# One attention head per 64-row half of the TensorE array, with dense matmuls as pairs of halves, in a gated mix of a Fourier layer and sliding-window attention

## The chip, the cores and the metric

The kernel runs on one core of one Trainium2 chip. The metric is device time in microseconds (us) of one execution. A core has TensorE (PE, with its weight loads shown apart as PEld), VectorE (DVE), ScalarE (ACT), GpSimd (POOL) and SyncE (SP), which issues all DMAs of this kernel. Each engine works its own queue in order and waits for semaphores of the others.

## The reference

For one sequence of 2048 tokens and 512 features, a gate mixes a Fourier layer (a) and a sliding-window attention (b):

```python
x = A_x
g = sigmoid((x * gate_w).sum(-1, keepdims=True))
# a: real part of the DFT over features, then over the sequence
re, im = x @ dft_hid_re.T, x @ dft_hid_im.T
a = dft_seq_re @ re - dft_seq_im @ im
# b: 32 heads of 16 features, each query sees itself and the 255 keys before it
q, k, v = split(x @ wqkv)
p = softmax(where(0 <= i - j < 256, q @ k.T / 4, -1e9))
b = (p @ v) @ wo
return g * a + (1 - g) * b
```

The weights of q, k and v are scaled up, so scores are large and float32 accuracy is needed.

## The kernel before

**Dense matmuls.** Every dense product is exact to near float32 by splitting both factors into a rounded part `hi` and a rest `lo` (type float32r, which PE takes in one pass) and adding three products (`TERMS`). A step of contraction over 128 is so three matmuls of 128x128 weights by 512 columns. There are 2496 of them ahead of the output projection: projections of q and k (`dqk`, `qk_proj`), of v (`dv`, `v_proj`), the DFT over features (`dab`, `ab_proj`), and the DFT over the sequence (`dc`, `c_block` and `c_pair`, 16 row blocks for the real and 16 for the imaginary part, 48 matmuls each). A piece of the DFT matrix is loaded as `raw` (128x1024), cast to `hi` and subtracted to `lo` on DVE (`load_split`, lines 82 and 83), two pieces for each row block. The output projection (`wo_block`, 192 matmuls) follows when the attention is done.

**Attention.** Heads are taken in 4 groups of 4 pairs, and queries in blocks of 64 (`BQ`, `NB` = 32 blocks in a group, 128 block steps in all). One matmul serves both heads of a pair: 64 rows of its result belong to one head, 64 to the other. To keep the heads apart, the weights are copies of the block (`make_pad`, three on DVE at line 304 and one on ACT at line 302 for each block) in which half of the contraction rows is zeroed. For block n and pair p:

- `s_pair`: scores s of the block's queries against a window of up to 320 keys (PE, line 319). A custom reduction on DVE (line 321) adds the mask and takes the row's minimum of -s into `nm`; ACT (line 324) takes the exponential and its row sums `l`.
- every 8 blocks `m_rows` and `l_rows` transpose the maxima and the reciprocal sums on PE, and DMAs carry the maxima through DRAM into rows 96 to 99 of `ring[0]`, so that they become part of a contraction.
- `t_pair`, `LAG` = 18 blocks later: the scores transposed, t, of the block's keys against up to 320 queries, with the maximum subtracted by those rows (PE, line 384). ACT takes the exponential into `pt` (line 385), POOL zeroes what lies outside the window (lines 390 and 394).
- `pv`, for two blocks at a time: P times V in plain float32, four passes of PE, with 32 columns of weights for each pair, so that four column parts of the array are in use (line 411).

**Order.** PE's order is written out by hand: the loop over n and p issues one s, one t (`k = n - LAG`) and then takes dense matmuls from the generator `dense()` at a fixed rate (`fill`, `FILL_*` matmuls for each p). We call one p a slot: s, t and 3 or 4 dense matmuls. ACT, DVE, POOL and SP are ordered by the scheduler of the language. PSUM has eight buffers of 128x512: four (`ps_a`) that s and t, and the transposes, take in turn, two for P times V (`ps_o`), two for dense results (`ps_d`). A matmul into a buffer waits until what read the buffer before is done: for s that is the reduction on DVE, for t the exponential on ACT.

## Time and profile before

| | |
|---|---|
| Runs | 880.5, 881.56, 883.99 us (median 881.56) |
| The profiled execution, span | 881.0 us |
| Matmuls on PE in the profile | 5184 |
| First and last s (line 319) | 35.0 and 672.4 us |
| Last t (line 384) | 754.7 us |

The profile gives for each engine its busy time, for stretches of time the busy time of every engine, for groups of instructions their count, busy time and mean duration, and in a timeline the start, duration and (in brackets) the idle time ahead of single instructions with what ended it. Matmuls overlap in a pipeline, so the distance between starts tells more than the duration: a dense matmul lasts 0.39 us, and the next begins long before it ends. Up to 35 us the first projections run, then the attention with dense matmuls between, and behind 755 us what is left of the DFT and the output projection.

### The profile page before, as it was taken

What the parts mean: (1) busy time and instruction counts of PE and PEld (TensorE: products, weight loads), DVE (VectorE), ACT (ScalarE), POOL (GpSimd) and SP (SyncE); (2) the same over time, 40 slices, a digit from 0 to 9 for tenths busy, and PEclk for the clock granted to TensorE, in tenths of its full rate; (3) what the DMA queues carried; (4) which work ended last, traced back from release to release, by engine and by line L of the source; (5) the groups of instructions that cost most, each with busy time, mean ns of one, the idle gap of its engine ahead of it and who ended that gap; (6) DMA issues with size and microseconds to landing.
All of it is one profiled execution on the core that took longest, in us unless ns stands there. A gap on an engine that the chain in (4) does not pass through costs nothing.

```text
span 881.0 us, 17206 instructions
## 1 busy us (share of the span) xinstructions
PE 867.3 (98%) x5184; PEld 690.6 (78%) x5184; DVE 604.8 (69%) x1965; ACT 590.3 (67%) x1794; POOL 384.9 (44%) x1069
## 2 busy tenths in 40 slices
PE   7999899999999999999999999999999999999998
PEld 5888677777777778787878787878777787788886
DVE  4688789777888678787877677778786433544342
ACT  5488789878889887888888878888786444101000
POOL 9100165554544446656456565745555665100000
PEclk9999999999999999999999999999999999999999
DMA  7877667675656126544444454469743424355453
GB/s 246 274 232 212 197 218 263 216 246 179 225 198 213 43 72 216 159 130 126 140 141 132 147 147 128 134 203 324 256 154 95 137 96 144 110 180 165 134 160 113
DMA packets 89822, 152.13 MB, mean 173 GB/s; under 512 B 26752, under 2 KB 35456, under 8 KB 89728
## 3 DMA queue, kind: packets, MB, share of 16 engines
q1 hardware_dynamic: 89728, 151.02, 54.6%
q8 instruction: 41, 0.67, 0.3%
q14 instruction: 53, 0.43, 0.2%
HBM read 103.81 MB, written 47.19 MB: 171 GB/s over the span
## 4 chain that ended last, share of the span: by engine, by line
PE 93%; DVE 2%; DMA 2%; ACT 1%; issue 0%; SPq 0%; ACTq 0%
PE dc L442 40%; PE s L319 9%; PE dab L260 9%; PE t L384 8%; PE dqk L238 8%; PE o L411 8%; PE t L604 5%; PE dv L260 5%; DMA qk_scr<-hl 1%; DMA pt<-xT 1%; DMA ab_scr<-hl 1%; DVE sm L321 1%; ACT sm L324 0%; PE s L343 0%; PE s L331 0%
## 5 line engine op out<-in xcount | busy, mean ns | idle before, releaser
L442 PE MATMUL dc<-big,hi 128*128 128x512 f32 x1024 | 341.0, 394 | 0.0
L390 POOL TENSOR_SCALAR_AFFINE_SELECT pt<-pt 64x128 f32<-64x128 f32 x512 | 195.4, 382 | 285.2 <-ACT pt L385 270.1
L321 DVE CUSTOM_DVE_ANT_0 sm<-s,mask 128x320 f32<-128x320 f32 (+4 forms) x512 | 232.6, 462 | 114.6 <-PE t L384 74.9
L324 ACT ACTIVATE sm<-sm,nm 128x320 f32<-128x320 f32 (+4 forms) x512 | 276.6, 541 | 25.8 <-DVE nm L321 21.7
L385 ACT ACTIVATE pt<-t 128x320 f32<-128x320 f32 (+4 forms) x512 | 210.8, 414 | 117.9 <-PE t L384 114.4
L442 PEld LDWEIGHTS dc<-big,hi 128*128 128x128 f32 x1024 | 189.4, 188 | 28.1
L442 PE MATMUL dc<-big,lo 128*128 128x512 f32 x512 | 201.6, 394 | 0.0
L384 PE MATMUL t<-ring,pad 128*128 128x320 f32 (+4 forms) x512 | 158.3, 309 | 3.8 <-ACT pad L302 2.8
L319 PE MATMUL s<-ring,pad 128*128 128x320 f32 (+4 forms) x512 | 160.4, 313 | 0.8 <-ACT pt L385 0.8
L394 POOL TENSOR_SCALAR_AFFINE_SELECT pt<-pt 64x128 f32<-64x128 f32 x448 | 157.1, 351 | 0.0
L304 DVE TENSOR_SCALAR pad<-ring,half 96x256 fp32r<-96x256 f32 x384 | 122.3, 365 | 27.4 <-PE t L384 26.2
L319 PEld LDWEIGHTS s<-ring,pad 128*128 128x128 f32 x512 | 96.2, 188 | 41.5 <-issue 7.4
L384 PEld LDWEIGHTS t<-ring,pad 128*128 128x128 f32 x512 | 96.4, 188 | 27.8 <-issue 3.2
L442 PEld LDWEIGHTS dc<-big,lo 128*128 128x128 f32 x512 | 96.3, 188 | 11.2
L83 DVE TENSOR_TENSOR lo<-raw,hi 128x512 fp32r<-128x512 f32 x146 | 99.5, 709 | 0.2 <-ACT hi L80 0.2
L324 ACT ACTIVATION_READ_ACCUMULATOR sm<-sm,nm 128x1 f32 x512 | 97.8, 191 | 0.0
L260 PE MATMUL dab<-hi,big 128*128 128x512 f32 x256 | 86.6, 395 | 0.2 <-DVE hl L88 0.2
L82 DVE CAST hi<-raw 128x512 fp32r<-128x512 f32 x142 | 57.8, 444 | 39.2 <-DMA raw<-ci 19.6
L238 PE MATMUL dqk<-big,hi 128*128 128x512 f32 x240 | 84.2, 398 | 0.0
L80 ACT CAST raw<-ev 128x512 fp32r<-128x512 f32 x16 | 9.9, 621 | 108.5 <-DVE lo L83 64.9
L411 PE MATMUL o<-pt,vpad 128*32 128x320 f32 (+4 forms) x1408 | 78.4, 352 | 0.0
L411 PEld LDWEIGHTS o<-pt,vpad 128*32 128x32 f32 x1408 | 35.9, 109 | 37.5 <-issue 18.0
(79 smaller groups left out, 823.4 us busy)
## 6 DMA issues: line engine op xcount, KB each, us to landing
qk_scr<-hl SPq DMA_DIRECT2D x32, 512.0 KB
ring<-qk_scr SPq DMA_DIRECT2D x32, 512.0 KB
raw<-cr SPq DMA_DIRECT2D x32, 512.0 KB
raw<-ci SPq DMA_DIRECT2D x32, 512.0 KB
ab_scr<-hl SPq DMA_DIRECT2D x20, 512.0 KB
big<-ab_scr SPq DMA_DIRECT2D x20, 512.0 KB
ring<-qk_scr SPq DMA_DIRECT2D x32, 256.0 KB
r_scr<-ev SPq DMA_DIRECT2D x25, 256.0 KB
```

The costliest lines, as they stand in the source:

```text
L238: nc.tensor.matmul(ps, w[a][:, c:c + 128], XT[dk, ss][:, b], start=n == 0, stop=n == 11)
L260: nc.tensor.matmul(ps, XT[dk, ss][:, a, c * 128:(c + 1) * 128], wh[b], start=n == 0, stop=n == 11)
L304: nc.vector.tensor_scalar(dst, src, half[:96, h:h + 1], None, op0=OP.mult)
L319: nc.tensor.matmul(ps[:, :w], PAD[0, n][:, p], ring[1][:, p, k0:k0 + w], start=True, stop=True)
L321: mark("dve", nc.vector.tensor_tensor_reduce(out=sm[:, :w], in0=ps[:, :w], in1=mask[:, WIN - w:], scale=1.0, scalar=3e38, op0=OP.add, op1= ...
L324: mark("act", nc.scalar.activation(sm[:, :w], sm[:, :w], AF.Exp, bias=nm[:, c], scale=-1.0, accum_out=l[:, c]))
L384: nc.tensor.matmul(ps[:, :w], PAD[1, n][:, p], ring[0][:, p, q0:q0 + w], start=True, stop=True)
L385: nc.scalar.activation(pt[:, p, :w], ps[:, :w], AF.Exp, scale=-1.0)
L390: nc.gpsimd.affine_select(a, a, pattern=[[0, 2], [1, 64]], compare_op=OP.is_ge, fill=0.0, base=0, channel_multiplier=-1)
L394: nc.gpsimd.affine_select(a, a, pattern=[[0, 2], [-1, 64]], compare_op=OP.is_gt, fill=0.0, base=0, channel_multiplier=1)
L411: nc.tensor.matmul(OT[g, sb][32 * p:32 * p + 32, q - sb * 512:e - sb * 512], v2[:, p], pt[:, p, q - q0:e - q0], start=first, stop=kb == 8 ...
L442: nc.tensor.matmul(ps, w[a][:, s8 * 128:(s8 + 1) * 128], ab[SC[i]][:, b], start=i == 0 and a + b == 0, stop=i == 15 and a == 1)
```

## The change

Attention takes one head at a time. Heads come in 8 groups (`NS`) of 4 (`NH`), and queries in blocks of 128, so there are again 128 block steps. `ring[0]` and `ring[1]` hold two heads one above the other: head h of a pair has rows 64 h to 64 h + 63 of all tiles. Its matmuls contract over 48 or 50 of these rows, which uses one half of the array's rows; the windows are 384 wide. s of a slot has the half p % 2 and t the other one (`t_head(k, p ^ 1)`).

While the attention runs (`rows[0]`), every dense matmul is issued as two, one for each half of the contraction rows, into two PSUM buffers (`mm`, `acc`); `collect` adds them with a copy on ACT and an add on DVE, and where a result is added to something anyway, a second instruction does so. Results begun before the attention keep whole matmuls.

The padded copies, the masks for them, and the exponential of s with its row sums are left out. V's weights for a head have 16 columns of v and 16 of ones, so P times V gives the row sums in its row 16. `pv` runs once for 512 queries; its result is copied from PSUM by ACT, and the sums go through DRAM to DVE for the reciprocal, and through DRAM again to all rows. PSUM: three buffers (not four) for s, t and transposes, one for P times V, four for dense results. `LAG` is 9 blocks, of twice the size.

```diff
-BQ = 64
-NB = S // BQ
-WIN = 320
+NS = 8
+NH = 4
+NB = S // P
+WIN = 384
-LAG = 18
+LAG = 9
-FILL_FIRST, FILL_PROJ, FILL_SEQ = 3.0, 3.5, 3.6
+FILL_FIRST, FILL_PROJ, FILL_SEQ = 4.0, 4.2, 4.25
...
-    ps_a = ctx.enter_context(tc.tile_pool(name="ps_a", bufs=4, space=PSUM))
-    ps_o = ctx.enter_context(tc.tile_pool(name="ps_o", bufs=2, space=PSUM))
+    ps_a = ctx.enter_context(tc.tile_pool(name="ps_a", bufs=3, space=PSUM))
+    ps_o = ctx.enter_context(tc.tile_pool(name="ps_o", bufs=1, space=PSUM))
...
+    def acc():
+        return [ps_d.tile([P, 512], F32, name=f"d{h}", tag=f"d{h}", bufs=2) for h in range(1 + rows[0])]
+
+    def mm(pss, w, x, start, stop):
+        if len(pss) == 1:
+            nc.tensor.matmul(pss[0], w, x, start=start, stop=stop)
+        else:
+            for h in range(2):
+                r = slice(64 * h, 64 * h + 64)
+                nc.tensor.matmul(pss[h], w[r], x[r], start=start, stop=stop)
+
+    def collect(pss):
+        if len(pss) == 1:
+            return pss[0]
+        t = ev.tile([P, 512], F32, name="es", bufs=3)
+        mark("act", nc.scalar.copy(t, pss[0]))
+        mark("dve", nc.vector.tensor_add(t, pss[1], t))
+        return t
...
-    def s_pair(n, p):
+    def s_head(n, j):
+        p, h = divmod(j, 2)
...
+        k0 = max(0, (jb - 2) * P)
+        w = (jb + 1) * P - k0
+        r = slice(64 * h, 64 * h + 48)
         ps = ps_a.tile([P, 512], F32, name="s", tag="st")
-        nc.tensor.matmul(ps[:, :w], PAD[0, n][:, p], ring[1][:, p, k0:k0 + w], start=True, stop=True)
-        sm = at.tile([P, WIN], F32, name="sm", bufs=3)
+        nc.tensor.matmul(ps[:, :w], ring[0][r, p, jb * P:(jb + 1) * P], ring[1][r, p, k0:k0 + w],
+                         start=True, stop=True)
+        sm = at.tile([P, WIN], F32, name="sm")
         mark("dve", nc.vector.tensor_tensor_reduce(out=sm[:, :w], in0=ps[:, :w], in1=mask[:, WIN - w:],
                                                    scale=1.0, scalar=3e38, op0=OP.add, op1=OP.min,
-                                                   accum_out=nm[:, c]))
-        mark("act", nc.scalar.activation(sm[:, :w], sm[:, :w], AF.Exp, bias=nm[:, c], scale=-1.0,
-                                         accum_out=l[:, c]))
+                                                   accum_out=ML[u][:, c:c + 1]))
...
+    def t_head(n, j):
...
+        r = slice(64 * h, 64 * h + 50)
         ps = ps_a.tile([P, 512], F32, name="t", tag="st")
-        nc.tensor.matmul(ps[:, :w], PAD[1, n][:, p], ring[0][:, p, q0:q0 + w], start=True, stop=True)
-        nc.scalar.activation(pt[:, p, :w], ps[:, :w], AF.Exp, scale=-1.0)
+        nc.tensor.matmul(ps[:, :w], ring[1][r, p, q0:q0 + P], ring[0][r, p, q0:q0 + w], start=True, stop=True)
+        mark("act", nc.scalar.activation(pt[:, j, :w], ps[:, :w], AF.Exp, scale=-1.0))
...
+            for j in range(NH):
+                nc.tensor.matmul(ot[32 * j:32 * j + 32, a - sb * 512:e - sb * 512], v2[:, j],
+                                 pt[:, j, a - kb * P:e - kb * P], start=kb == kbs[0], stop=kb == kbs[-1],
                                  skip_group_check=True)
...
+        os = at.tile([P, 512], F32, name="os")
+        nc.scalar.copy(os, ot)
+        ls = l_scr[u]
+        ld(ls[0], os.rearrange("(j r) s -> j r s", r=32)[:, 16])
+        lt = at.tile([P, 16], F32, name="lt", bufs=1)
+        ld(lt, ls[0].rearrange("j (a b) -> (j a) b", b=16))
+        nc.vector.reciprocal(lt, lt)
+        ld(ls[1].rearrange("j (a b) -> (j a) b", b=16), lt)
+        rl = at.tile([P, 512], F32, name="rl", bufs=1)
+        ld(rl, bass.AP(tensor=ls.tensor, offset=ls[1].offset, ap=[[512, NH], [0, 32], [1, 512]]))
+        nc.vector.tensor_mul(rl, os, rl)
...
         for p in range(NH):
             if n < N:
-                s_pair(n, p)
+                s_head(n, p)
             if 0 <= k < N:
-                t_pair(k, p)
+                t_head(k, p ^ 1)
+                if p % 2:
+                    t_mask(k, p // 2)
             fill(n)
```

How the order of the engines changes is shown at two places. The first is PE in the middle of the attention, during the DFT over the sequence; before, a slot reads like this, with P times V (`o`) ahead of it (the numbers behind names count tiles):

```order
L411 MATMUL o<-pt,vpad_312 32x64 x4
L411 MATMUL o<-pt,vpad_312 32x256 x4
L411 MATMUL o<-pt,vpad_311 32x320 x4
L319 MATMUL s<-ring_252,pad_0_245 128x320
L384 MATMUL t<-ring_251,pad_0_248 128x320
L442 MATMUL dc<-big,hi 128x512
L442 MATMUL dc<-big,lo 128x512
L442 MATMUL dc<-big,hi 128x512 x2
L319 MATMUL s<-ring_252,pad_1_246 128x320
L384 MATMUL t<-ring_251,pad_1_249 128x320
```

And after (`d` are the dense results, two tiles for one result), two slots, with what each instruction waits for; here P times V is not shown:

```order
L305 MATMUL s<-ring_284,ring_283 128x384 [waits Activation_49]
L358 MATMUL t<-ring_283,ring_284 128x384 [waits DVE_49]
L202 MATMUL d_2166<-hi,big 128x512
L202 MATMUL d_2167<-hi,big 128x512
L202 MATMUL d_2166<-hi,big 128x512
L202 MATMUL d_2167<-hi,big 128x512
L202 MATMUL d_2166<-lo,big 128x512
L202 MATMUL d_2167<-lo,big 128x512
L202 MATMUL d_2166<-hi,big 128x512
L202 MATMUL d_2167<-hi,big 128x512
L305 MATMUL s<-ring_284,ring_283 128x384 [waits Activation_49]
L358 MATMUL t<-ring_283,ring_284 128x384 [waits DVE_49]
```

The operands of s and t are now the ring itself and not padded copies, dense matmuls stand in pairs, and with three buffers it is t that waits for DVE, and s for ACT. The second place is DVE in the DFT over the sequence, where pieces of the DFT matrix are split. Before (`sm,nm` is the reduction of s, with the row that reads its minimum behind it):

```order
L82 CAST hi<-raw 128x512 x2
L321 ISA sm,nm<-s,mask 128x320
L321 ISA nm 128x1
L83 TENSOR_TENSOR lo<-raw,hi 128x512 x2
L321 ISA sm,nm<-s,mask 128x320
L321 ISA nm 128x1
L304 TENSOR_SCALAR pad_1_246<-ring_251,half 96x4x64 x2
L304 TENSOR_SCALAR pad_1_249<-ring_252,half 96x4x64
L321 ISA sm,nm<-s,mask 128x320
```

After, at a like place (`ev` is the second half of a dense result):

```order
L308 ISA sm,nm<-s,mask 128x384
L308 ISA nm 128x1
L83 CAST hi<-raw 128x512 x2
L84 TENSOR_TENSOR lo<-raw,hi 128x512 x2
L532 SCALAR_TENSOR_TENSOR ev<-d_5505,g_305,ev 128x512
L308 ISA sm,nm<-s,mask 128x384
L308 ISA nm 128x1
L308 ISA sm,nm<-s,mask 128x384
L308 ISA nm 128x1
```

The padded copies are gone from between the reductions, and casts, subtractions and the second eviction of a dense result stand in one run between two of them.

## The prediction

> **What bounds the kernel now.** I read the head of the page, then the chain of waits, then one stretch of a hundred microseconds by engine.

> ```profile
> span 881.0 us, 17206 instructions
> PE 867.3 (98%) x5184; PEld 690.6 (78%) x5184; DVE 604.8 (69%) x1965; ACT 590.3 (67%) x1794; POOL 384.9 (44%) x1069
> PE 93%; DVE 2%; DMA 2%; ACT 1%; issue 0%; SPq 0%; ACTq 0%
> 400.00:500.00 100.00, 100.00 (x639) 79.01 (x638) 79.11 (x269) 82.10 (x255) 55.19 (x149) 1.00 0.44 135
> ```

> The last row gives span, then busy time of PE, PEld, DVE, ACT and POOL. PE has no gap while DVE and ACT are idle for a fifth: work taken from ACT, DVE or POOL alone is worth nothing here, and what counts is the time between starts on PE. The profiled 881.0 stands 0.56 under the median of 881.56, so the sum holds for both. The starts of one slot (one s, one t and its dense matmuls), in the timeline of PE:

> ```profile
> 405.56 0.31 PE L319 MATMUL s<-ring,pad 128*128 128x320 f32 x1
> 405.70 0.31 PE L384 MATMUL t<-ring,pad 128*128 128x320 f32 x1
> 405.86 0.63 PE L442 MATMUL dc<-big,hi 128*128 128x512 f32 x2
> 406.32 0.39 PE L442 MATMUL dc<-big,lo 128*128 128x512 f32 x1
> 406.55 0.40 PE L442 MATMUL dc<-big,hi 128*128 128x512 f32 x1
> 406.79 0.31 PE L319 MATMUL s<-ring,pad 128*128 128x320 f32 x1
> ```

> A dense matmul of 512 columns takes 0.235 from start to start (406.32 to 406.79, two), s or t of 320 columns 0.145 (405.56 to 405.86, two). Both are some 0.455 ns a column. A slot with four dense ones is 1.23.

> **s and t.** Columns of all s: 4 pairs x 4 groups x 9,600 = 153,600 of 320-wide windows (narrower at the edge), so s and t together cost 2 x 153,600 x 0.455 ns = 139 us. After, 184,320 columns each (384-wide), but s stands in one half of the rows and the t behind it in the other. If the halves run side by side, a pair costs what one does: 184,320 x 0.455 ns = 84, and 36 slots at each end have an s or a t alone, 36 x 0.175 = 6 more: 90. **Term: -49.** Not side by side it would be 168, +29. That parts of the array do run side by side, the P times V group shows, for column parts:

> ```profile
> L411 PE MATMUL o<-pt,vpad 128*32 128x320 f32 (+4 forms) x1408 | 78.4, 352 | 0.0
> 400.51 0.40 PE L442 MATMUL dc<-big,hi 128*128 128x512 f32 x1
> 400.83 1.29 PE L411 MATMUL o<-pt,vpad 128*32 128x64 f32 x24
> 402.05 0.41 PE L319 MATMUL s<-ring,pad 128*128 128x320 f32 x1
> 402.30 0.31 PE L384 MATMUL t<-ring,pad 128*128 128x320 f32 x1
> ```

> 1408 of 352 ns each fit into 78.4 us. No row of before shows row parts; I take them as overlapping likewise.

> **The dense matmuls.** 2364 of 2496 become pairs; 132 ahead of the first s and the 192 of the output projection stay whole. If a pair costs what the whole one did, 0.235, nothing changes, and that is the value I take. It can't be below, since each half streams the same 512 columns. Above, if the halves ran one after the other, 2364 x 0.235 = +555. Between lies the load of weights, which twice as many instructions now need. What one load takes at least, a short t shows:

> ```profile
> 751.02 0.19 PE L384 MATMUL t<-ring,pad 128*128 128x64 f32 x1
> 751.04 0.48 PE L442 MATMUL dc<-big,lo 128*128 128x512 f32 x1
> 751.37 0.63 PE L442 MATMUL dc<-big,hi 128*128 128x512 f32 x2
> ```

> From the t to the second dense one are 0.35; less 0.235 for the first dense one, the t took 0.115, though 64 columns are 0.03: that is the floor set by loading 128 columns of weights. Two loads in turn are 0.23, just inside a pair's 0.235, but s beside t would cost 0.23 in place of 0.175: 512 x 0.055 = +28, a rival below. Term: 0, with 0 to 555 as ends.

> [...]

> **P times V and the rows of maxima.** The batch of 640 columns above holds PE from 400.83 to 402.05, the dense one ahead lasts 0.32 in place of 0.235, and the s behind it 0.25 in place of 0.145: 1.41 in all, of which 640 x 4 passes x 0.455 ns = 1.17 (four column parts at once) is streaming and 0.24 the switch. Before, 64 batches of 600 columns in the mean: 64 x (1.09 + 0.24) = 85. After, 32 batches of 1440: 32 x (2.62 + 0.24) = 92. **Term: +7.** 33 transposes of maxima replace 16 of maxima and 16 of sums: 0.

> **What leaves ACT and DVE.** The second exponential with its row sums (L324), the padded copies (L302, L304) and their memsets go. PE waited for none of it in the stretch above, so this is 0. In return each dense result inside the attention is a copy on ACT and an add on DVE more, and the maximum covers 384 keys:

> ```profile
> L304 DVE TENSOR_SCALAR pad<-ring,half 96x256 fp32r<-96x256 f32 x384 | 122.3, 365 | 27.4 <-PE t L384 26.2 <-DMA ring<-qk_scr 1.0
> L321 DVE CUSTOM_DVE_ANT_0 sm<-s,mask 128x320 f32<-128x320 f32 x448 | 212.7, 483 | 100.6 <-PE t L384 73.8 <-PE s L319 22.0 <-ACT sm L324 3.3
> L321 DVE CUSTOM_DVE_ANT_0 sm<-s,mask 128x256 f32<-128x256 f32 x16 | 6.6, 418 | 2.1 <-PE t L384 1.1 <-PE s L319 0.6 <-ACT sm L324 0.4
> L88 DVE TENSOR_TENSOR hl<-dqk,hl 128x512 fp32r<-128x512 f32 x15 | 10.3, 684 | 2.2 <-ACT hl L86 2.2
> ```

> DVE: -122 for the pads; 65 ns more on 448 reductions (483 less 418 for 64 columns), +29; 69 adds and 32 second evictions at 0.68, +69; 32 products of 0.68 with the sums in place of 16, +11: within some 15 us of what it was. As a sum it still fits. When its work comes is another matter.

> **The wait that is added.** s and t took turns in four PSUM buffers and now have three. So t of slot p+1 lands in the buffer of s of slot p, and waits for that s's reduction; before, only the s two slots on did. Behind a waiting t on PE stand all dense pairs of the slot and the next P times V. The times:

> ```profile
> 409.00 0.31 PE L319 MATMUL s<-ring,pad 128*128 128x320 f32 x1
> 409.46 0.49 DVE L321 CUSTOM_DVE_ANT_0 sm<-s,mask 128x320 f32<-128x320 f32 x1 [0.53 <-PE t L384]
> 406.39 0.47 DVE L321 CUSTOM_DVE_ANT_0 sm<-s,mask 128x320 f32<-128x320 f32 x1
> 406.80 0.07 DVE L321 DVE_READ_ACCUMULATOR2_ANT nm<- 128x1 f32 x1
> 406.80 0.48 DVE L321 CUSTOM_DVE_ANT_0 sm<-s,mask 128x320 f32<-128x320 f32 x1
> 405.09 1.38 DVE L83 TENSOR_TENSOR lo<-raw,hi 128x512 fp32r<-128x512 f32 x2
> 403.82 0.94 DVE L82 CAST hi<-raw 128x512 fp32r<-128x512 f32 x2
> ```

> A reduction starts 0.46 after its s (409.00, 409.46) and holds DVE 0.41 (406.39 to 406.80); with 64 columns more 0.50 and 0.48, and its result stands 0.55 after its start. So s at 0 frees DVE at 0.98. If X is what DVE has in its queue before the next reduction, that one ends at 0.98 + X + 0.55. The t that needs it is due two slots after the first s, at 2 x (4 x 0.235 + 0.175) = 2.23, or up to 0.47 later where a slot holds five pairs (110 of 508 do). So X up to 0.65 to 0.9 costs nothing, and all above it stops PE. With four buffers it was one slot more, about 2.2.

> X from the order of DVE's queue: of 475 gaps between reductions behind the first 36, 228 are empty, 133 hold one instruction up to 0.65 (an lo is 1.30 / 2, a cast 0.4), 22 lie below 1.2, 38 between 1.2 and 1.9, and 54 above, 2.48 in the mean (two casts and two lo of a split piece are 2.1, with an add, product or eviction beside them 2.7 and more). At 0.65 all gaps together exceed the room by 133 us; the 54 alone, at 0.9, by 54 x 1.58 = 85. The ends are 0 (every gap finds PE late anyway) and 133; I take 85, since the middle gaps meet five-pair slots and P times V in part. **Term: +85.** Before, the same kind of gap hardly ever passed 2.2, which agrees with PE's 100.00 busy.

> [...]

> POOL has 480 mask operations of 256 elements in place of 960 of 128, in a batch that is used two slots later: 0, or up to 0.5 on each of 32 batches if late. The output projection stands in one piece at the end, but PE has its 45 us of work there as before: 0.

> **Sum:** 881 - 49 + 0 + 7 + 85 = **924**.

> **The rivals.** (1) It does what it says: DVE's gaps are covered, 881 - 49 + 7 = 839, up to 876 with some waits. For it: DVE's total does not grow, and PE was never stopped before by gaps of 2.1. Against it: the buffer that covered them is gone. It decides from 43 us of waits downwards. (2) Weights load one after another: +28, 952. For it: the floor of 0.115. Against it: the column parts load 1408 sets without such a cost. (3) SP's queue becomes late. Each batch now has a chain of DMAs through DRAM in order (sums out, in, reciprocals out, in, product out), and SP stood so before:

> ```profile
> SPq L55 <- DMA m_scr<-mhl: 34.2, 15, 4.8
> ```

> 2.3 us a time; three such for each of 32 batches are 220 us, behind which the loads of DFT pieces wait. If a late piece keeps a cast, and with it the reductions, from starting in a fifth of the 96 cases, that is 19 x 2.3 = +44, 968. (4) Row halves don't overlap for these types: 924 + 555 = 1479, and 1557 if s and t do not overlap either (168 in place of 90); already 0.253 for a pair undoes the 49 less 7.

> **How the numbers follow.** Forecast 0.44, rival 1 0.30, 2 0.12, 3 0.09, 4 0.05. A measurement of this kernel tells about 0.5% from no change. Rival 1 gives faster 0.27 and same 0.03; the others are slower, 0.70. The likeliest case's own range is 895 to 955; to hold the others it goes from 838 to 985.

> **What would show it.** Right: idle on PE before t, put down to the DVE reduction, some 50 to 100 times at 1 to 2 us, in slots where DVE casts a DFT piece; PE no longer at 100 in the middle; dense pairs 0.235 apart; s and t within 0.02 of each other. Wrong: PE without idle time and a span under 860 (rival 1); s to the next dense pair over 0.22 (rival 2); SP late and casts that wait for raw (rival 3); pairs at 0.47 (rival 4).

## The result, and the profile after

The changed kernel takes 1214.12 us (median of 4 runs, 1207.49 to 1216.86) where the kernel before takes 881.82 on the same chip: a ratio of 1.376, interval 1.371 to 1.380. The direction was forecast, the size was not: 1214 lies far above the range of 838 to 985. One execution among those reported below, the profiled one of e1_defer, took 2840 us and is left out together with its profile.

The head of the page of the changed kernel: span, busy time by engine, and PE's busy tenths and granted clock in 40 slices.

```profile
span 1215.0 us, 20586 instructions
PE 955.3 (79%) x7550; PEld 787.9 (65%) x7550; DVE 616.8 (51%) x1728; ACT 364.2 (30%) x734; POOL 229.8 (19%) x526
PE   7997887777778878777778877768777777799587
PEclk9998888788889888888888888889788888999799
```

No engine is full any more: PE, at 98% before, is busy for 79% and has 260 us without work, and DVE is at 51%. So the time is in waits between the engines. In the same stretch of 100 us as before (span, then PE, PEld, DVE, ACT, POOL, granted clock, DMA share, GB/s), PE has 22 us of gaps and the clock is at 0.86:

```profile
400.00:500.00 100.00, 77.64 (x662) 64.67 (x660) 53.61 (x154) 32.01 (x66) 20.24 (x48) 0.86 0.41 110
```

Who waits for whom (engine and line, what it waited for: us in total, times, longest), from the view of waits:

```profile
DVE rl L396 <- DMA rl<-l_scr: 147.7, 27, 9.4
PE t L358 <- DVE nm L308: 136.2, 54, 6.9
DVE lt L392 <- DMA lt<-l_scr: 96.4, 31, 7.4
PE s L305 <- DVE nm L308: 85.3, 38, 6.8
```

PE waits for the reductions on DVE (`nm`, 221 us), which the prediction expected at 85. But DVE itself is idle for 244 us at two lines of the division: the reciprocal (L392) and the product (L396) wait for their DMAs. (At the product 32 us more, in the other 5 of its 32 times, are put down to no DMA.) One such place in the timelines of DVE, SP and PE (start, duration, engine, line, operation, tile, and in brackets the idle time ahead of it and what ended it). First DVE:

```profile
515.23 0.76 DVE L83 CAST hi<-raw 128x512 fp32r<-128x512 f32 x2
515.90 1.28 DVE L84 TENSOR_TENSOR lo<-raw,hi 128x512 fp32r<-128x512 f32 x2
519.75 0.25 DVE L392 RECIPROCAL lt<-lt 128x16 f32<-128x16 f32 x1 [2.57 <-DMA lt<-l_scr]
519.92 0.66 DVE L532 SCALAR_TENSOR_TENSOR ev<-d,g,ev 128x512 f32<-128x512 f32 x1
520.50 0.55 DVE L308 CUSTOM_DVE_ANT_0 sm<-s,mask 128x384 f32<-128x384 f32 x1
...
526.51 0.69 DVE L396 TENSOR_TENSOR rl<-os,rl 128x512 f32<-128x512 f32 x1 [4.12 <-DMA rl<-l_scr]
527.12 0.55 DVE L308 CUSTOM_DVE_ANT_0 sm<-s,mask 128x384 f32<-128x384 f32 x1
```

Then the chain of transfers, as SP issues it:

```profile
514.35 0.52 SPq L56 DMA_DIRECT2D l_scr<-os  x1
...
516.57 0.34 SPq L56 DMA_DIRECT2D lt<-l_scr  x1
...
520.03 0.34 SPq L56 DMA_DIRECT2D l_scr<-lt  x1
...
521.49 0.54 SPq L56 DMA_DIRECT2D rl<-l_scr  x1
527.23 0.31 SPq L56 DMA_DIRECT2D u_scr<-rl  x1
```

And PE:

```profile
514.37 0.34 PE L305 MATMUL s<-ring,ring 48*128 48x384 f32 x1
514.37 0.34 PE L358 MATMUL t<-ring,ring 50*128 50x384 f32 x1
514.54 0.62 PE L202 MATMUL d<-big,hi 64*128 64x512 f32 x4
515.00 0.39 PE L202 MATMUL d<-big,lo 64*128 64x512 f32 x2
...
521.11 0.68 PE L305 MATMUL s<-ring,ring 48*128 48x384 f32 x1 [3.19 <-DVE nm L308]
521.11 0.69 PE L358 MATMUL t<-ring,ring 50*128 50x384 f32 x1
521.59 1.06 PE L202 MATMUL d<-big,hi 64*128 64x512 f32 x4
522.45 0.63 PE L202 MATMUL d<-big,lo 64*128 64x512 f32 x2
522.87 1.06 PE L202 MATMUL d<-big,hi 64*128 64x512 f32 x4
523.73 0.52 PE L358 MATMUL t<-ring,ring 50*128 50x384 f32 x1
...
527.74 0.68 PE L358 MATMUL t<-ring,ring 50*128 50x384 f32 x1 [2.36 <-DVE nm L308]
```

Read them together. SP issues the load of the sums at 516.57. DVE finishes a split of a DFT piece at 517.2 and comes to the reciprocal, whose data land at 519.7. The reduction behind it, of an s that PE had finished long before, starts at 520.50. PE's next s needs the buffer which that reduction empties, and goes on at 521.11 after 3.19 us without work. Five pairs then take from 521.59 to 523.73, 0.43 each and not 0.23 as at 514.54 to 515.00: the granted clock is 1.00 from 517.35 to 520.76, while PE stands, and 0.50 from 520.76 to 524.17. At 526.51 the same happens at the product. The first kind comes 31 times, the second 27, over 32 batches of P times V.

**An account of the attention.** For each stretch from one start of t to the next I took off what its instructions take undisturbed by the prediction's own prices (0.2335 for a dense matmul or pair, 0.455 ns a column of s and t, of the wider one where they stand side by side, and P times V at its streaming and 0.24). What is left is called the overrun:

| Kernel | first t | last t | overrun between | behind the last t | span |
|---|---|---|---|---|---|
| before | 99.4 | 754.7 | 3.5 | 126.3 | 881.0 |
| after | 78.8 | 1113.9 | 342.0 | 101.1 | 1215.0 |

So 1035 us of attention, with 2163 dense pairs in it in place of 1821 dense matmuls, would be 693 undisturbed. The account is good to some 5 us, since the price of a slot whose s and t stand apart is a choice.

### The profile page after: what moved, and what is told of

Same layout as the page of the kernel before. It is cut to its first block, busy times and chain, and to the rows that moved or that the text cites. A ratio compares the mean times of both kernels' runs of the same rounds, so it can differ in the third digit from the quotient of the medians.

```text
span 1215.0 us, 20586 instructions
## 1 busy us (share of the span) xinstructions
PE 955.3 (79%) x7550; PEld 787.9 (65%) x7550; DVE 616.8 (51%) x1728; ACT 364.2 (30%) x734; POOL 229.8 (19%) x526
## 5 line engine op out<-in xcount | busy, mean ns | idle before, releaser
L202 PE MATMUL d<-big,hi 64*128 64x512 f32 x2496 | 534.0, 430 | 1.4 <-DVE ev L547 1.4
L359 ACT ACTIVATE pt<-t 128x384 f32<-128x384 f32 (+2 forms) x512 | 240.3, 470 | 553.9 <-PE t L358 406.8
L202 PEld LDWEIGHTS d<-big,hi 64*128 64x128 f32 x2496 | 371.4, 209 | 15.6 <-issue 3.6
L202 PE MATMUL d<-big,lo 64*128 64x512 f32 x1248 | 357.4, 431 | 0.0
L308 DVE CUSTOM_DVE_ANT_0 sm<-s,mask 128x384 f32<-128x384 f32 (+2 forms) x512 | 261.8, 524 | 116.0 <-PE s L305 98.7
L358 PE MATMUL t<-ring,ring 50*128 50x384 f32 (+2 forms) x512 | 202.3, 395 | 137.5 <-DVE nm L308 136.2
L364 POOL TENSOR_SCALAR_AFFINE_SELECT pt<-pt 128x256 f32<-128x256 f32 x256 | 114.4, 447 | 794.6 <-ACT pt L359 794.6
L305 PE MATMUL s<-ring,ring 48*128 48x384 f32 (+2 forms) x512 | 187.1, 365 | 85.6 <-DVE nm L308 85.3
L202 PEld LDWEIGHTS d<-big,lo 64*128 64x128 f32 x1248 | 212.2, 209 | 6.9 <-issue 1.9
L202 PE MATMUL d<-hi,big 64*128 64x512 f32 x656 | 138.2, 426 | 0.0
L396 DVE TENSOR_TENSOR rl<-os,rl 128x512 f32<-128x512 f32 x32 | 22.4, 699 | 179.9 <-DMA rl<-l_scr 147.7
L368 POOL TENSOR_SCALAR_AFFINE_SELECT pt<-pt 128x256 f32<-128x256 f32 x224 | 100.4, 448 | 0.0
L83 DVE CAST hi<-raw 128x512 fp32r<-128x512 f32 x142 | 58.4, 452 | 27.6 <-PE d L202 18.0
L209 DVE TENSOR_TENSOR es<-d,es 128x512 f32<-128x512 f32 x69 | 47.5, 688 | 29.7 <-ACT es L208 26.2
```

The costliest lines, as they stand in the source:

```text
L83: nc.vector.tensor_copy(hi, raw)
L202: nc.tensor.matmul(pss[h], w[r], x[r], start=start, stop=stop)
L209: mark("dve", nc.vector.tensor_add(t, pss[1], t))
L305: nc.tensor.matmul(ps[:, :w], ring[0][r, p, jb * P:(jb + 1) * P], ring[1][r, p, k0:k0 + w], start=True, stop=True)
L308: mark("dve", nc.vector.tensor_tensor_reduce(out=sm[:, :w], in0=ps[:, :w], in1=mask[:, WIN - w:], scale=1.0, scalar=3e38, op0=OP.add, op1= ...
L358: nc.tensor.matmul(ps[:, :w], ring[1][r, p, q0:q0 + P], ring[0][r, p, q0:q0 + w], start=True, stop=True)
```

## The experiments

All ratios are to the kernel before on the same chip, with 95% intervals where there were several runs.

### Where the 342 us come from: e2_no_norm, e12_sp_only

The first leaves the division by the row sums out, with its transfers; P times V goes on undivided.

```diff
-        ls = l_scr[u]
-        ld(ls[0], os.rearrange("(j r) s -> j r s", r=32)[:, 16])
...
-        nc.vector.reciprocal(lt, lt)
...
-        nc.vector.tensor_mul(rl, os, rl)
...
-        ld(us[g % 4].rearrange("j r s -> (j r) s"), rl)
+        ld(us[g % 4].rearrange("j r s -> (j r) s"), os)
```

> Left out: the division by the row sums, with its four DMAs through DRAM, the reciprocal and the product; the undivided result is stored. Theory A: as the run with deferred division or a little faster, 890 to 980. Theory B and C: over 1130.

Measured in one run: 935.86 us; span 934.2, granted clock 0.989. Its page, and its slots in PE's timeline:

```profile
span 934.2 us, 20311 instructions
PE 873.5 (94%) x7550; PEld 711.2 (76%) x7550; DVE 599.4 (64%) x1664; ACT 363.8 (39%) x734; POOL 237.7 (25%) x526
```

```profile
508.58 0.34 PE L305 MATMUL s<-ring,ring 48*128 48x384 f32 x1
508.63 0.34 PE L358 MATMUL t<-ring,ring 50*128 50x384 f32 x1
508.76 0.45 PE L202 MATMUL d<-big,lo 64*128 64x512 f32 x2
509.00 0.68 PE L202 MATMUL d<-big,hi 64*128 64x512 f32 x4
509.46 0.45 PE L202 MATMUL d<-big,lo 64*128 64x512 f32 x2
...
514.19 0.44 PE L305 MATMUL s<-ring,ring 48*128 48x384 f32 x1 [0.77 <-DVE nm L308]
```

s and t together take 0.18 (508.58 to 508.76), a pair 0.23 (509.00 to 509.46, two). The division and its chain are worth 278 of the 332 us that the change lost; the overrun falls from 342.0 to 82.4. What is left is of the kind that was forecast, as at 514.19, where DVE had this in its queue:

```profile
510.83 0.76 DVE L83 CAST hi<-raw 128x512 fp32r<-128x512 f32 x2
511.50 1.49 DVE L84 TENSOR_TENSOR lo<-raw,hi 128x512 fp32r<-128x512 f32 x2
512.92 0.74 DVE L523 SCALAR_TENSOR_TENSOR ev<-d,g,ev 128x512 f32<-128x512 f32 x1
513.58 0.54 DVE L308 CUSTOM_DVE_ANT_0 sm<-s,mask 128x384 f32<-128x384 f32 x1
```

That run took out DVE's wait, SP's chain of transfers and the work itself at once. The second keeps every transfer of the chain in SP's queue, each waiting for the landing of the one before it, and both DVE instructions, but these read the copied P times V tile, so that the division is left out, DVE waits for no transfer, and the two stand a few reductions earlier in its queue:

```diff
-        nc.vector.reciprocal(lt, lt)
+        nc.vector.reciprocal(at.tile([P, 16], F32, name="lu", bufs=1), os[:, :16])
...
-        nc.vector.tensor_mul(rl, os, rl)
+        nc.vector.tensor_mul(at.tile([P, 512], F32, name="os"), os, os)
```

> The changed kernel with every DMA of the division left in SP's queue, in the same chain through DRAM and with all of SP's waits, but the two DVE instructions no longer wait for it: the reciprocal and the product read the copied P times V tile, so that the division is left out. Theory, DVE stands in its own order at these two instructions while the transfers run: the stops of PE go, 920 to 960, near the 936 of the run without the chain, and PE's clock is 0.97 or more. Rival, SP's queue standing at the chain is what is late (the third rival of the prediction): nothing of that is changed, 1180 to 1230.

Measured: 995.4 (2 runs), ratio 1.128 [1.125, 1.130]. It lies between the two ranges expected, 35 above the first and 185 below the second, so neither theory is the whole and the run sizes both. SP still stands at the chain, now by itself, in its view of waits and in its timeline:

```profile
SPq L56 <- DMA rl<-l_scr: 144.1, 32, 5.4
```

```profile
505.85 0.53 SPq L56 DMA_DIRECT2D l_scr<-os  x1
...
510.18 0.33 SPq L56 DMA_DIRECT2D lt<-l_scr  x1
...
518.36 0.34 SPq L56 DMA_DIRECT2D u_scr<-rl  x1
...
521.03 0.99 SPq L56 DMA_DIRECT2D raw<-cr  x2
```

From its first transfer to its last the chain takes 12.5 us here (505.85 to 518.36), and over the 32 batches 11.7 in the mean, against 12.9 in the changed kernel. SP's queue is thus held almost as long, and yet PE loses little by it: the overrun is 127.0. The sign of the third rival, casts that wait for a piece of the DFT matrix, is small in both: 3.8 us in all in the changed kernel, 14.9 here. From 342.0 to 127.0, 215 us, is DVE standing at the two lines; from 127.0 to 82.4, 45 us, is the work of the division on DVE and SP's chain together, which no run separates. The rest of the difference to the changed kernel is behind the last t: 101.1, 95.4 here, 81.5 without the division.

### The same division, put later in DVE's queue: e1_defer, e5_defer_more, e3_defer_split

Nothing is left out here. In e1 DVE's reciprocal stands half a batch (two blocks, eight slots) behind its P times V, and the product half a batch behind that:

```diff
-        nc.vector.reciprocal(lt, lt)
+    def norm1(u):
...
+        with behind("dve"):
+            nc.vector.reciprocal(lt, lt)
...
+            if p == 1 and k % 4 == 2 and k >= 6:
+                norm1(k // 4 - 1)
...
+                if k >= 8:
+                    norm2(k // 4 - 2)
```

> The reciprocal of the row sums is issued 8 slots behind its load and the product 8 slots behind the loads of the reciprocals, both behind that slot's reduction on DVE; nothing else changes. Theory A (DVE, in order, stands still at these two instructions until their DMAs land, 276 us of idle before them, and PE stops behind the reductions queued after them): the idle before both falls under 40 us, PE's waits for the reduction fall from 222 us to under 100, the granted clock rises from 0.88 to over 0.95, and the time falls by 200 us or more, to 900 to 1000. Theory B (the third buffer alone: any run of casts and subtractions stops PE): the time stays over 1130. Theory C (pairs of halves draw the clock down by themselves): the time and the clock of 0.88 stay within 3%.

Measured: 989.04 (3 runs), ratio 1.119 [1.116, 1.122]; 225 us won by order alone, that of the two instructions and of the transfers that follow them. The clock of 0.968 to 0.972 is as theory A expected; what it expected of the idle time is not known. In e5 the product stands a whole batch behind the reciprocal:

```diff
+                if k >= 10:
+                    norm2(k // 4 - 2)
...
-                if k >= 8:
-                    norm2(k // 4 - 2)
```

> The product is deferred by 8 slots more than in the first deferral, to a whole batch behind the reciprocal, three buffers in turn as in the change. If what the first deferral (989) kept over the run without division (936) is DVE still standing at the product until its load lands (61.7 us of idle there, 20 times, in the run with divided buffers): 930 to 960, and that idle under 10 us. If it is the DMAs themselves or SP's queue: 975 to 1000.

Measured: 979.4 (2 runs), ratio 1.110 [1.108, 1.113]. From its view of waits:

```profile
DVE rl L410 <- DMA rl<-l_scr: 31.8, 4, 9.4
DVE lt L400 <- DMA lt<-l_scr: 19.6, 7, 4.9
```

That is 51 us in place of 244; the overrun is 104.8, and 101 us still lie behind the last t, where the last batch's division has nothing to hide behind. So most of the price was not that of the division, whose DVE work and bytes are all there, but of its place. The time itself is in the range that was given to the DMAs or SP's queue (975 to 1000), and the idle at the product did not fall under 10 us. But all four waits at the product start behind 825 us, with the last batches; of the 42 us between the spans of e2_no_norm and e5, 22 are overrun and 20 lie behind the last t. e3 is e1 with the three buffers given out as two for s and one for t:

```diff
-        ps = ps_a.tile([P, 512], F32, name="s", tag="st")
+        ps = ps_a.tile([P, 512], F32, name="s", tag="st", bufs=2)
...
-        ps = ps_a.tile([P, 512], F32, name="t", tag="st")
+        ps = ps_a.tile([P, 512], F32, name="t", tag="t", bufs=1)
```

> As the deferred division, and the three PSUM buffers are divided: two for s and the transposes, one for t, so that t waits for the exponential on ACT of the t before, and s for the reduction two slots back. If the bank wait of the prediction (85 us) is real beside theory A: 60 to 110 us below the deferred division alone. If the bank wait is hidden: within 15 us of it. If t's single buffer is a new stop: slower by up to 50 us.

Measured: 975.45, ratio 1.105 [1.103, 1.107], 14 below e1. Within 15 us was what had been expected if the wait for a buffer were hidden; it is not hidden, for s still waits 39.5 us for the reduction, and a part of the wait moves to t, which now waits for its exponential (20.5 us). This division of the buffers does not take it away.

### The buffers alone, in the kernel before: e4_before_3

```diff
-    ps_a = ctx.enter_context(tc.tile_pool(name="ps_a", bufs=4, space=PSUM))
+    ps_a = ctx.enter_context(tc.tile_pool(name="ps_a", bufs=3, space=PSUM))
```

> The kernel before with three buffers in place of four for s, t and transposes. If three buffers in turn cost by the gaps on DVE (theory B, at the predicted size): 940 to 990. If the wait is hidden: within 10 us of 881.

Measured in one run: 899.23, 16 above the kernel before; the overrun goes from 3.5 to 19.7. That is neither hidden (within 10 us) nor the predicted size (940 to 990). So the fourth buffer is worth 16 us with before's queue on DVE and its slots; the rest of the 82 must come with what else was changed, the shorter slots and the longer, differently ordered work on DVE, which no run takes apart.

### What is left without the division: e6_act_cast, e7_act_split, e8_fill, e9_spread, e11_tail

e6 is e5 with the casts of DFT pieces on ACT (the subtractions stay on DVE), e7 is e6 with buffers as in e3, e8 is e6 with fewer dense matmuls in a slot:

```diff
-                    w[cc, j] = load_split((cr, ci)[cc][j // 2, j % 2])
+                    w[cc, j] = load_split((cr, ci)[cc][j // 2, j % 2], True)
...
-FILL_FIRST, FILL_PROJ, FILL_SEQ = 4.0, 4.2, 4.25
+FILL_FIRST, FILL_PROJ, FILL_SEQ = 4.0, 4.0, 3.7
```

> As the longer deferral, and the casts of the DFT pieces are done by ACT in place of DVE, which shortens DVE's runs between two reductions: over 0.65 us they sum to 102 in place of 140 us. If the bank wait is what keeps PE from 100%: 20 to 40 us less than the longer deferral. If not: within 10 us of it, or slower if ACT holds up t's exponential.

> As the run with casts on ACT, with two PSUM buffers for s and one for t. Bank wait theory: another 10 to 40 us less, to about 880 to 900. If t's one buffer stops PE behind ACT's casts: 5 to 40 us more than the run with casts on ACT.

> As the run with casts on ACT, with fewer dense matmuls in a slot (4.0 and 3.7 in place of 4.2 and 4.25), so that some ten row blocks of the DFT are left behind the attention, with the output projection between them. In the run without division the output projection in one piece took 63 us for 45 us of matmuls. If that tail and not the attention is at fault: 15 to 25 us less than the run with casts on ACT; shorter slots give a little back to the bank wait.

Measured: e6 962.07, ratio 1.089 [1.085, 1.093], overrun 92.4; 17 below e5, a little less than the 20 to 40 expected. e7 954.17, ratio 1.082 [1.079, 1.084], overrun 87.7; 8 below e6, again less than the 10 to 40 expected. It is the fastest of those that keep the division, with 35.6 us of PE's waits now at t for the exponential, for which t has one buffer. e8 995.05, ratio 1.128 [1.125, 1.130], a loss of 33 where a gain of 15 to 25 was expected. Shorter slots end the attention 11.5 us earlier (850.9 in place of 862.4) but leave some 40 us more of dense work behind it: with less PE work in a slot the same work of DVE leaves more open, the overrun goes from 92.4 to 132.2.

e9 is e5 with the casts and subtractions of DFT pieces handed out one a slot, each behind that slot's reduction; e11 is e9 with the last batch's division put between blocks of dense work, which a lower rate of dense matmuls (`FILL_SEQ`) leaves over for it. Of both edits a part is shown:

```diff
+            drop()
...
+    def drop():
+        if drip:
+            with behind("dve"):
+                drip.pop(0)[1]()
```

```diff
-FILL_FIRST, FILL_PROJ, FILL_SEQ = 4.0, 4.2, 4.25
+FILL_FIRST, FILL_PROJ, FILL_SEQ = 4.0, 4.2, 4.1
...
+    attention_done()
+    ahead(10)
     norm2(30)
     norm1(31)
+    ahead(22)
     norm2(31)
-    attention_done()
```

> Against the run with the product deferred by a whole batch (979): casts and subtractions of the pieces of the DFT over the sequence are handed out one a slot, behind that slot's reduction, and the pieces are loaded two ahead. Theory, what is left in the attention is the wait for a PSUM buffer at long stretches of other work on DVE: the stretches over 0.65 us add up to 80 us of excess in place of 140 by the order of DVE's queue, so 920 to 950. Rival, what is left comes from the masks and exponentials (PE waiting for ACT and POOL) or from the tail: 965 to 985.

> The run with the pieces handed out one a slot, and beside it the end of the program rearranged: the last batch's division is put between blocks of dense work that is left over for it, so that its transfers lie beside PE, and the output projection follows. Theory, the 101 us behind the last t can be 80, as in the run without division: 15 to 25 below the run with the pieces handed out alone. Rival, the tail is set by the transfers of the last batch itself and not by their place: within 5 us of that run.

Measured: e9 958.24, ratio 1.084 [1.082, 1.087], 21 below e5 and not the 29 at least that the theory of long stretches on DVE gave; the overrun only went from 104.8 to 92.8. e11 964.74, ratio 1.094 [1.087, 1.101]: no gain, and 15 to 25 us were expected. The attention has 12 us less dense work and is only 6 shorter (785.5 to 779.8), and behind the last t there are 15 more (92.0 to 107.4). Its theory fell.

Why taking the long stretches away won so little can be read from the starts. In e2_no_norm 150 slots run over by 0.15 us or more, 98 us together; in 140 of them an s or a t starts within 0.3 us of the end of a reduction, which fits the wait for a buffer. (About half of the slots that do not run over have such a start as well, so the count supports it and does not prove it.) Only 22 us of it stand behind stretches of more than 1.6 us on DVE, 24 behind a single instruction of up to 0.8 (an add of second halves among them), and 43 behind a reduction that directly follows another: DVE works off what piled up.

### Whole dense matmuls beside s and t in halves: e10_whole

e5 with one line taken out, so that no dense matmul is split:

```diff
-    rows[0] = True
```

> Against the run with the product deferred by a whole batch (979): the dense matmuls stay whole, 128 rows and one instruction, and s and t stay in halves of 64 rows; ACT's copies and DVE's adds of second halves go. Theory, going between halves and whole rows costs PE about what P times V shows for column parts (0.24 a batch for two changes): 508 slots at 0.19 are 97 us, less what DVE wins by 69 adds (some 20 us): 1040 to 1070. Rival, the change of shape costs nothing and the pairs were not needed: 930 to 975, since DVE has less to do.

Measured: 1066.38 (2 runs), ratio 1.208 [1.206, 1.211], 87 above e5. PE's share of busy time, and two slots in its timeline:

```profile
PE 1041.0 (98%) x5186; PEld 610.5 (57%) x5186; DVE 563.8 (53%) x1627; ACT 335.5 (32%) x674; POOL 240.3 (23%) x526
```

```profile
502.81 0.44 PE L305 MATMUL s<-ring,ring 48*128 48x384 f32 x1
502.81 0.44 PE L358 MATMUL t<-ring,ring 50*128 50x384 f32 x1
503.18 0.73 PE L198 MATMUL d<-big,hi 128*128 128x512 f32 x2
503.75 0.40 PE L198 MATMUL d<-big,lo 128*128 128x512 f32 x1
503.99 0.39 PE L198 MATMUL d<-big,hi 128*128 128x512 f32 x1
504.31 0.44 PE L305 MATMUL s<-ring,ring 48*128 48x384 f32 x1
```

A slot with four dense matmuls takes 1.50 (502.81 to 504.31) where 4 x 0.235 + 0.175 = 1.115 are work. Over all 511 stretches 190 us are left over, 0.37 each: the price of going from whole rows to halves and back. It is paid by PE at 98% busy and clock 0.995, without a wait for DVE: slots so long cover the buffers. 190 more for the switch and 105 less for the waits make the 87 of e10 over e5. The range expected (1040 to 1070) held by luck: the switch cost 0.37 a slot and not 0.19, and the 105 us of waits went away, where the expectation took off some 20 for the adds. The pairs, at 0.23 like a whole matmul, save the switch. The loads of weights show it too: in the view of waits the load of an s stands behind 0.36 us without a load, 362 times, for which the profile shows no releaser:

```profile
PEld s L305 <- issue: 131.5, 362, 0.4
```

In the changed kernel, where the dense matmuls ahead of it are pairs, such idle time ahead of the load of s is 1.1 us in all.

## Why the prediction was wrong, by its steps

**s and t side by side (-49), pairs (0), P times V (+7): right.** Without the division an undisturbed execution would be 77 to the first t, 693 to the last and some 64 behind it, 834 us; the terms gave 881 - 49 + 7 = 839. Pairs are 0.23 apart, s and t 0.17 to 0.18 together, batches of P times V within 6 us of the account in all. Rivals 2 and 4 fall with that. That a pair costs what a whole matmul does is shown by no run of before; it was an assumption, and the runs gave the 0.23. The prediction counts four passes for P times V, 1.82 ns a column; the traces give 1.7: from the start of a batch to the matmul behind it are 0.79 us for 384 columns (608.48 to 609.27) and 1.22 for 640 (400.83 to 402.05) before, 1.96 for 1152 (102.72 to 104.68) and 2.61 for 1536 (136.88 to 139.49) after. So the split of a batch into streaming and 0.24 is an estimate; measured is the batch as a whole.

**What leaves ACT and DVE (0): right.** In e2_no_norm PE waits neither for the exponentials on ACT nor for POOL's masks.

**The bank wait (+85): right in size, and partly by luck.** The overrun without the division is 82.4. But I took the 54 long gaps for all of it; they are a quarter, and the rest lies in short gaps and in reductions one behind the other, which I had priced at nothing. So the size came out by one part put too high and others left out. (The room was worked out a little short as well: 2.23 - 0.98 - 0.55 is 0.70 and not 0.65.)

**The output projection (0): too low by some 17.** Behind the last t there are 81.5 us for some 64 of work in e2_no_norm, where PE waits 9 us for casts of the attention's own output on ACT (`ACT raw`), which themselves wait for loads from DRAM, and 101 in the changed kernel, with the last batch's division ahead of it.

**The division: the step that failed.** Its chain of transfers was seen, and called rival 3: but it was put on SP's queue, where a load of a DFT piece stands behind it, at 2.3 us in a fifth of 96 cases, +44. On DVE the prediction counted its products by their duration (+11) and did not ask what they wait for. DVE works its queue in order, and the reciprocal and the product stand in it ahead of reductions for which PE waits; there they cost 3.1 and 5.5 us idle each time (96.4 / 31 and 147.7 / 27) against 0.65 to 0.9 that PE can spare by the prediction's own count. Measured: 215 us in the attention, a wait that the sum had at nothing. Rival 3 and the work of the division together cost the remaining 45. That this is near rival 3's 44 is chance: the 45 hold the DVE work too, and casts waited for pieces no more than 3.8 us in the changed kernel and 14.9 in e12_sp_only.

**What a stop costs: missing from the sum.** Of the 221 us between e12_sp_only and the changed kernel 60 are not idle but slower streaming (PE's busy time, as the profile models it, of 895 and 955 for the same matmuls): after stops of 2.36 and 3.19 us the pairs take 0.43 (521.59 to 523.73, five). The granted clock is at half for 287 of the 1215 us of the changed kernel and for 73 of the 994 of e12_sp_only.

The signs named for a right forecast were there, t waiting for the reduction 54 times, but at 2.5 us in the mean and not 1 to 2, and in slots with a division as well as those with a DFT piece. That alone would not have told the two causes apart; the runs did.

None of these versions beats the kernel before: the best, e7, stays 8% above it. By the account it has an overrun of 88 and some 30 behind the last t beyond the work there; 72 of these 118 would have to go. A further PSUM buffer for s and t was not tried: the eight that the program has are all given out.

## What to carry to other kernels

For each instruction that a change adds to an engine that works in order, ask first what it waits for and who stands behind it, and only then how long it runs: a reciprocal and a product of 0.9 us together cost some 7 us of PE's time a batch (215 us over 32), because transfers came in ahead of them. The room is that of the tightest consumer behind it (here up to 0.9 us by the prediction's count, set by PSUM buffers), and the chain of transfers through DRAM took many times that here (12.9 us): issue it, let half a batch or more of other work go by, and read it then. The waits that stopped TensorE here (3.19 and 2.36 us at the place shown) cost more than themselves, since a granted clock of 0.5 followed them: 60 of 221 us were slower streaming.
